# Weight pieces that are swapped inside a segment loop, loaded by one transfer or by two of half the columns

## The chip, the cores and the metric

The kernel runs on one core of a Trainium2 chip. The metric is the device time of one execution in microseconds (us). TensorE (PE) does the matrix products, VectorE (DVE), ScalarE (ACT) and GpSimd (POOL) the rest, and SyncE (SP) issues transfers, which 16 DMA engines carry out. The profile comes from one execution, recorded by the hardware profiler.

## What is computed

Two branches over the same input of 2048 tokens by 640 are mixed with a gate for each token, `g * a + (1 - g) * b`. Branch `b` is a gated feed-forward network. Branch `a` is attention with a recurrent memory: 64 segments of 32 tokens, where each segment's first 8 output rows are the memory of the next. Cut to what matters:

```python
mem = mem0
for s in range(n_seg):                       # 64
    h = jnp.concatenate([mem, xs], axis=1)   # 8 + 32 rows
    q, k, v = h @ Wq, h @ Wk, h @ Wv         # 640 -> 32 heads x 192, each
    p = softmax(mask(q @ k.T * scale))
    o = (p @ v) @ Wo                         # 32 x 192 -> 640
    mem = o[:, :M, :].copy()
    outs.append(o[:, M:, :])
```

The segments therefore run one after another, and each needs all four weight matrices (bf16, 7.5 MB each).

## The kernel before

**Stages.** First the feed-forward branch runs over four blocks of 512 tokens, and its result goes to DRAM (`b_scr`). Then six units of the so-called left part (the last 8 tokens of each segment, whose Q and K do not depend on the memory) are prepared, and then `segment(s)` runs 64 times.

**Pieces.** The weights are cut into pieces. A key `(m, o, k)` with m = 0, 1, 2 is a slab of Wq, Wk or Wv: 128 rows of the 640 (one k of KT = 5) by the 1536 columns of eight heads (an "octet", o = 0 to 3), 384 KB. A key `(3, p)` is one of 16 pieces of Wo, 128 by 1920, 480 KB. The 76 pieces together do not fit into the on-chip memory. So 13 pieces of octet 0 share their place (a "slot") with the same piece of octet 3, and Wo pieces 0, 1, 2 with 13, 14, 15 (`partner`, lines 545 to 552). Even segments go through octets 0, 1, 2, 3, odd ones through 3, 2, 1, 0. Within a segment the first octet's pieces are used first, and then their slots are loaded with the partner, which the same segment uses last and the next segment first. That is a swap. In every segment from 1 on, 16 pieces are swapped: 5 of Wk, 3 of Wq, 5 of Wv, 3 of Wo; in segment 0 there are eight.

**Order.** `PROG` (line 506) is the order of one segment, written out by hand: `("g", n, k)` are the projections of group n (`proj`, whose matmuls are recorded at L1046, and at L226 where the weights stay loaded), `sc`, `ex`, `pt`, `pv` the attention of one octet, `wo` the output projection (`wo_part`: L1206, and L1229 for the last octet), `lf`, `le`, `vb` the left part for later segments. After each item, `swap_loads(s, item)` (line 612) looks at the pieces just used and calls `load_piece` (line 597) for the partner of each that has one; the K pieces of the first group wait until that group's last item.

**Queues.** All transfers of the segment loop are issued by SP in the order in which the program adds them: the swaps (L599), the output of the segment before (`out_store`, L956), the next segment's input (`x_load`, L706), the next segment's left Q and K (`stg_load`, L935), the feed-forward result (`bz_load`, L947; every fourth segment also `bzl_load`, L952), stores of the left part (L895, L1276). An issue waits on SP until what it overwrites has been read; what stands behind it waits as well.

**Waits.** `_Sched.add` works out the dependencies from regions of memory. A transfer raises the semaphore of its slot by 16 when it has landed, and a matmul that reads a piece waits for the latest value that any write to an overlapping region will reach. `finalize` leaves out a wait that an earlier one on the same engine covers. Each projection matmul reads columns from the whole width of its piece: four matmuls of one piece, each with every fourth group of 32 columns (Q, K) or a quarter of the columns (V).

## Time and profile before

Three runs took 1762.07, 1763.03 and 1769.55 us; the median is 1763.03. The profiled execution's span is 1765.1 us.

| What | Value |
|---|---|
| Median of 3 runs | 1763.03 us |
| Span of the profiled execution | 1765.1 us |
| Mean granted TensorE clock | 0.994 of full speed |
| Feed-forward and preparation, until the first full segment | about 210 us |
| One segment | 22.4 to 27.8 us between first swaps |
| Moved by DMA | 499.57 MB, 283 GB/s over the span |
| Transfers of Wq, Wk, Wv, Wo in the whole run | 209, 335, 335, 205 |
| Median time from issue to landing of these | 5.4, 7.1, 9.1, 6.4 us |

In lines of the profile, a group of instructions is named by the line of the kernel that recorded it, its engine and its operands, `out<-in`; `arena` is the on-chip memory that holds all weights and working tiles, `ps` the accumulators. In the views of waits the columns are the waiting engine and line, whom it waited for, the total in us, how often, and the longest. In the views of the DMA engines the digits are the busy share of 40 equal slices of the window in tenths. In the timeline of SP the columns are the start in us, the time of the issues together, the line, and the number of issues merged into one row.

### The profile page before, as it was taken

Reading aid. Unit: us, or ns where it says so; the run is one execution under the profiler, and the core shown is the slowest. Engines: PE = TensorE matmul, PEld = TensorE weight load, DVE = VectorE, ACT = ScalarE, POOL = GpSimd, SP = SyncE. Lnnn points to the kernel's source line nnn. Section 1 sums busy time; section 2 is a strip of 40 time slices with the busy share of each in tenths; the row PEclk is TensorE's granted clock in tenths of the full one; section 3 lists DMA queues with packets and bytes.
Section 4 is the critical chain, followed back from the end, with each engine's and each line's share of the span. In section 5 each row is a group of like instructions: output and inputs, shape, how many; then the busy total and the mean of one; then the engine's idle time right before and its main releaser. Section 6 shows DMA issues by size and latency. Waiting matters only on the chain.

```text
span 1765.1 us, 80301 instructions
## 1 busy us (share of the span) xinstructions
PE 1623.9 (92%) x39162; PEld 809.5 (46%) x31501; DVE 960.0 (54%) x2932; ACT 802.8 (45%) x1835; POOL 320.0 (18%) x1099
## 2 busy tenths in 40 slices
PE   9999999999999999999999989999999998999887
PEld 4554444444444444454444444454444444454444
DVE  2222655556555655555555655555555655655554
ACT  3222544545444544444444544444444544445443
POOL 1100111111112112111212111111211121121211
PEclk9999999999999999999999999999999999999999
DMA  9814987888778887888788887879787886879776
GB/s 335 295 48 157 329 313 250 320 313 288 280 269 311 299 308 253 315 290 319 281 280 293 296 293 250 314 285 323 279 280 275 311 310 241 312 282 327 283 275 238
DMA packets 271311, 499.57 MB, mean 283 GB/s; under 512 B 105304, under 2 KB 132208, under 8 KB 270960
## 3 DMA queue, kind: packets, MB, share of 16 engines
q1 hardware_dynamic: 267832, 491.34, 78.3%
q8 instruction: 276, 4.52, 1.0%
q10 hardware_dynamic: 3128, 3.09, 0.6%
q14 instruction: 75, 0.61, 0.1%
HBM read 473.22 MB, written 21.11 MB: 280 GB/s over the span
## 4 chain that ended last, share of the span: by engine, by line
PE 71%; DVE 15%; DMA 6%; issue 4%; ACT 4%; DVEq 0%; SPq 0%; ACTq 0%
PE ps L1046 20%; PE ps L226 15%; PE ps L1206 8%; DMA arena<-in_A_Wo_dram 5%; PE ps L1177 3%; PE ps L804 3%; PE ps L801 3%; PE ps L884 3%; PE ps L1100 3%; PE ps L819 2%; PE ps L1087 2%; DVE ps L1114 2%; DVE arena L1112 2%; PE ps L1095 2%; PE ps L1229 2%
## 5 line engine op out<-in xcount | busy, mean ns | idle before, releaser
L1046 PE MATMUL ps<-arena 128*32 128x384 bf16 x9940 | 723.0, 329 | 42.4 <-DVE arena L1375 34.4
L226 PE MATMUL ps<-arena 128*32 128x384 bf16 x7680 | 595.4, 328 | 7.9 <-DVE arena L1215 3.5
L1046 PEld LDWEIGHTS ps<-arena 128*32 128x32 bf16 x9940 | 257.5, 97 | 365.3 <-issue 226.0
L1080 DVE STREAM_TRANSPOSE arena<-arena 128x384 bf16<-128x384 bf16 x512 | 270.8, 557 | 150.8 <-ACT arena L1066 149.2
L1066 ACT ACTIVATE arena<-ps 128x384 bf16<-128x384 f32 x512 | 236.2, 489 | 211.6 <-PE ps L1046 196.3
L1206 PE MATMUL ps<-arena 128*32 128x320 bf16 x6144 | 293.6, 301 | 13.9 <-issue 13.4
L1124 ACT ACTIVATE ps<-ps 104x160 f32<-104x160 f32 x256 | 71.9, 281 | 293.4 <-DVE ps L1114 293.4
L1206 PEld LDWEIGHTS ps<-arena 128*32 128x32 bf16 x6144 | 163.5, 97 | 74.0 <-issue 19.4
L1112 DVE TENSOR_REDUCE arena<-ps 104x4 f32<-104x160 f32 x256 | 83.0, 324 | 165.8 <-PE ps L1100 164.6
L941 POOL COPY arena<-arena 128x96 bf16<-128x96 bf16 x256 | 70.3, 275 | 513.4 <-PE ps L1100 444.2
L1188 ACT ACTIVATE arena<-ps 128x480 bf16<-128x480 f32 (+1 forms) x256 | 137.0, 535 | 43.8 <-PE ps L1179 39.6
L1196 POOL COPY arena<-arena 128x96 bf16<-128x96 bf16 x256 | 68.3, 267 | 441.1 <-ACT arena L1188 357.3
L1162 ACT ACTIVATE arena<-ps 128x448 bf16<-128x448 f32 x192 | 104.2, 543 | 96.7 <-PE ps L1149 96.4
L1069 ACT ACTIVATE arena<-ps 128x384 bf16<-128x384 f32 x256 | 125.1, 489 | 20.9 <-PE ps L1046 16.3
L1177 PE MATMUL ps<-arena 128*64 128x160 bf16 x1536 | 123.1, 243 | 12.5 <-ACT arena L1162 6.9
L1126 DVE TENSOR_REDUCE arena<-ps 104x4 f32<-104x160 f32 x256 | 83.0, 324 | 92.5 <-ACT ps L1124 92.5
L1177 PEld LDWEIGHTS ps<-arena 128*64 128x64 bf16 x1536 | 80.8, 109 | 91.6 <-issue 31.7
L884 PE MATMUL ps<-arena 128*32 128x384 bf16 x1280 | 111.4, 330 | 2.2 <-issue 2.0
L1179 PE MATMUL ps<-arena 128*64 128x64 bf16 x1536 | 104.8, 193 | 4.1 <-issue 4.1
L891 DVE STREAM_TRANSPOSE arena<-arena 128x384 bf16<-128x384 bf16 x128 | 73.7, 576 | 31.6 <-ACT arena L889 27.8
L1215 DVE TENSOR_TENSOR arena<-ps,arena 64x160 f32<-64x160 f32 x160 | 50.8, 317 | 72.3 <-ACT arena L1212 61.6
L1114 DVE TENSOR_TENSOR ps<-ps,arena 104x160 f32<-104x160 f32 x256 | 85.0, 332 | 8.8
(84 smaller groups left out, 1819.2 us busy)
## 6 DMA issues: line engine op xcount, KB each, us to landing
arena<-in_A_Wk_dram SPq DMA_DIRECT2D x335, 384.0 KB, 7.1
arena<-in_A_Wv_dram SPq DMA_DIRECT2D x335, 384.0 KB, 9.1
arena<-in_A_Wo_dram SPq DMA_DIRECT2D x205, 480.0 KB, 6.4
arena<-in_A_Wq_dram SPq DMA_DIRECT2D x209, 384.0 KB, 5.4
arena<-left_qk_scratch SPq DMA_DIRECT2D x126, 96.0 KB, 2.8
left_qk_scratch<-arena SPq DMA_DIRECT2D x49, 192.0 KB, 2.3
left_qk_scratch<-arena SPq DMA_DIRECT2D x30, 96.0 KB, 5.7
ffn_b_scratch<-arena ACTq DMA_DIRECT2D x16, 160.0 KB, 4.4
```

Of the source, the lines that this page charges most:

```text
L226: return e.add_instruction(mybir.InstMatmult(name=nm, start_tensor_calc=like["start"], stop_tensor_calc=stop, tile_size=(128, 32), tile_po ...
L884: fns.append(lambda e, outp=outp, rhs=rhs, j=j: e.matmul(outp, lhs, rhs, start=(k == 0), stop=(k == KT - 1), tile_position=(0, 32 * j)))
L1046: fns.append(lambda e, outp=outp, rhs=rhs, j=j: e.matmul(outp, lhs, rhs, start=(k == 0), stop=(k == KT - 1), tile_position=(0, 32 * j)))
L1066: S_.add("act", lambda e, m=m, bk=bk: e.activation(out=rows_sb[m], in_=ps[:, bk, 0:384], func=ACTF.Copy), reads=[r_ps[bk]], writes=[r_rows ...
L1069: S_.add("act", lambda e, i=i, bk=bk: e.activation(out=v_sb[i % NVB].rearrange("p (c n) -> p c n", c=3), in_=ps[:, bk, 0:384].rearrange("p ...
L1080: S_.add("dve", lambda e: e.transpose(out=dst[:, :, 0:L], in_=rows_sb[m].rearrange("p (c r) -> p c r", r=L)), reads=[r_rows[m]], writes=[r ...
L1112: S_.add("dve", lambda e: e.tensor_reduce(out=mxs, in_=S3, axis=AX.X, op=ALU.max), reads=[rb], writes=[rst], name="smax max")
L1114: S_.add("dve", lambda e: e.tensor_tensor(out=S3, in0=S3, in1=mxb, op=ALU.subtract), reads=[rb, rst], writes=[rb], name="smax sub")
L1177: return [lambda e: e.matmul(full, v[:, e0:e0 + 64], PTm[:, i], start=True, stop=False, tile_position=(0, 64 * i), skip_group_check=True), ...
L1179: lambda e: e.matmul(part, vl[:, e0:e0 + 64], PTl[:, i], start=False, stop=True, tile_position=(0, 64 * i), skip_group_check=True)]
L1188: S_.add("act", lambda e: e.activation(out=apx(u[:, 0, 0, :], [[R, na], [3 * R, 4], [1, R]]), in_=ps[:, A, 0:na * W].rearrange("p (c t r) ...
L1206: fns.append(lambda e, i=i, t=t, j=j, gv=gv: e.matmul(ps[32 * j:32 * j + 32, bank, 0:2 * DJ].rearrange("p (h n) -> p h n", h=2), lhs2[i], ...
```

## The change

`load_piece` is called for the first loads (`"res"`) and for the swaps (`"swap s..."`). The first loads stay as they are. A swap is now two transfers with the same semaphore, one for each half of the piece's columns; each half has a region of its own, half as wide, so a reader of the piece depends on both. For Wo the two inner dimensions (3 x 640) are flattened to 1920 columns first. A half's row in one partition is 1536 bytes for Wq, Wk and Wv (3072 before) and 1920 bytes for Wo (3840 before).

```diff
     def load_piece(key, name):
         loaded[slot_id[key]] = key
-        S_.add("sp", lambda e: e.dma_start(piece_view(key, res_off[key]), piece_src(key)), writes=[r_res[key]],
-               dma_sem="slot%d" % slot_id[key], name="%s %s" % (name, key))
+        if not name.startswith("swap"):
+            S_.add("sp", lambda e: e.dma_start(piece_view(key, res_off[key]), piece_src(key)), writes=[r_res[key]],
+                   dma_sem="slot%d" % slot_id[key], name="%s %s" % (name, key))
+            return
+        n = piece_size(key) // 2
+        dst, src = bview(res_off[key], 2 * n), piece_src(key)
+        if key[0] == 3:
+            src = src.rearrange("p c n -> p (c n)")
+        for x in range(2):
+            S_.add("sp", lambda e, x=x: e.dma_start(dst[:, n // 2 * x:n // 2 * (x + 1)], src[:, n // 2 * x:n // 2 * (x + 1)]),
+                   writes=[sreg(res_off[key] + n * x, n)], dma_sem="slot%d" % slot_id[key], name="%s %s %d" % (name, key, x))
```

## The prediction

> **What bounds the kernel now.** I read the page first (busy shares, chain), then the DMA queues over the segment loop, then who waits for a weight load, and last the order of one segment on SP's queue. By "late" I mean time against the schedule of before.

> ```profile
> span 1765.1 us, 80301 instructions
> PE 1623.9 (92%) x39162; PEld 809.5 (46%) x31501; DVE 960.0 (54%) x2932; ACT 802.8 (45%) x1835; POOL 320.0 (18%) x1099
> ...
> PE 71%; DVE 15%; DMA 6%; issue 4%; ACT 4%; DVEq 0%; SPq 0%; ACTq 0%
> ```

> The span is TensorE's: it is busy for 92% of it and fills 71% of the chain. A load enters the chain with 6% only. So a slower load costs nothing until it lands after the matmul that wants it. The next view (busy time by stretches, the segment loop alone; the last two columns are DMA share and GB/s) shows how near that is, and the waits of TensorE's weight loads and matmuls show that it already happens:

> ```profile
> 228.00:1765.00 1537.00, 1404.86 (x36808) 700.77 (x29456) 881.47 (x2754) 728.02 (x1696) 295.18 (x1026) 0.99 0.81 290
> ```

> ```profile
> PEld ps L1229 <- DMA arena<-in_A_Wo_dram: 8.6, 12, 2.5
> PEld ps L1046 <- DMA arena<-in_A_Wk_dram: 2.0, 5, 0.7
> PEld ps L1046 <- DMA arena<-in_A_Wv_dram: 0.4, 1, 0.4
> ```

> The 16 DMA engines are 81% busy on average in the loop, and PE waits about 11 us in all for weights, mostly for the third Wo piece, the last swap of a segment. In one segment the DMA share by slices, and SP's issues, stand like this:

> ```profile
> DMA  5488999999999999999999999999999999977430
> ...
> q1 hardware_dynamic: 3153, 6.93, 91.1%
> ```

> ```profile
> 918.86 0.33 SPq L599 DMA_DIRECT2D arena<-in_A_Wk_dram  x1
> 919.36 1.29 SPq L599 DMA_DIRECT2D arena<-in_A_Wq_dram  x3
> 920.69 1.92 SPq L599 DMA_DIRECT2D arena<-in_A_Wk_dram  x4
> 922.66 2.51 SPq L599 DMA_DIRECT2D arena<-in_A_Wv_dram  x4
> 925.21 0.57 SPq L956 DMA_DIRECT2D out_dram<-arena  x1
> 925.83 0.51 SPq L706 DMA_DIRECT2D arena<-x_scratch  x1
> 926.38 1.00 SPq L599 DMA_DIRECT2D arena<-in_A_Wv_dram  x1
> 930.89 1.84 SPq L599 DMA_DIRECT2D arena<-in_A_Wo_dram  x3
> ```

> The reader is to see that 13 pieces of 384 KB are issued in 8.5 us, while the engines work them off until about 937, without a gap; the three Wo pieces join the end of the same backlog. From the trace's landing times, the median distances from landing to first use are, by s % 4: for the fifth V piece 2.60 / 1.01 / 0.91 / 1.91 us (s%4 = 0, 1, 2, 3), for the third Wo piece 1.81 / 0.04 / 0.50 / 2.57 us. 0.04 is a matmul that waited. So half of the segments have no slack, the other half about 2 us.

> **The change, part by part.**

> *Packets.* Every swap (8 in segment 0, 16 in each of the 63 others: 1016 transfers) becomes two. The bytes stay. Each transfer has one packet for each of 128 partitions, 8 to an engine, and one 4-byte semaphore packet to an engine. The medians of the trace's packet records are 9 ns for 4 bytes, 36 for 768, 55 for 1280, 121 for 3072 and 149 for 3840. From 3072 to 3840 the slope is 28 / 768 = 0.0365 ns a byte, and a line through 3072 leaves 121 - 112 = about 8.5 ns that do not depend on the size (768 bytes: 28 + 8.5 = 36.5, agrees). No packet of 1536 bytes is in the trace; by the line it takes 64.5 ns, bounds from the nearest rows 55 (1280) and 121 / 2 = 60.5 (no fixed part) below, 72 (the 95th percentile at 1280) above. A piece then costs 8 x 8.5 + 9 = 75 to 77 ns more on each engine; I take 75. The bounds give 9 ns (only the semaphore) and 8 x 23 + 9 = 190 ns. That the packets are really back to back is seen in the backlog: landings of 384 KB pieces are 0.95 to 0.98 us apart, and 8 x 121 + 9 = 977 ns. Thus by the last V piece (the 13th) the engines are 13 x 0.075 = 0.98 us late, by the third Wo piece 16 x 0.075 = 1.2 us.
> [...]

> *Issues.* SP issues 16 more transfers in a segment. The second half has no wait of its own: it writes what the same matmuls released, and both raise the slot's one semaphore, for whose last value the matmul waits. An issue of a swap takes 0.436 us (median of 992 in the loop) or 0.528 (mean; the long ones lie mainly where nine and more transfers are outstanding), and 0.045 to the next. Whether a half costs the median or the mean decides which is slower, SP or the engines. From the first Wk issue to that of the last V half there are 25 intervals plus out store and x load (0.57 + 0.51 + 0.09 = 1.17 us): 25 x 0.481 + 1.17 = 13.2 us, or 25 x 0.573 + 1.17 = 15.5. A first piece lands 3.93 us after its issue (mean of 62 segments), 2.95 more than its own 0.98, so the last V half lands 13.2 + 2.95 + 0.53 = 16.7 or 19.0 us after the first issue. Before, it lands at 17.28 (mean), and the engines alone make that 18.26. So SP is hidden under the engines at the median and adds 19.0 - 18.26 = 0.74 us at the mean. I take the middle, 0.36: last V 1.33 us late, third Wo 1.56. What is queued behind on SP: the Wo swaps, then stg_load, bz_load, bzl_load, the left stores. Before, SP stands idle from 937.2 to 940.7 in the segment shown, so these slip by 1 to 2 us into idle time; POOL's fill of the next segment's Q and K has over 3 us until its scores. I cost them at nothing; without that cover they would add their lag beyond it, under 1 us a segment.

> *The sum.* Per segment, PE is pushed by the largest of (lateness - slack) over its 16 pieces, and the next segment starts afresh, because its first swap is released by PE itself. Over the 62 segments from 230 us on, with each segment's own slacks: s%4 = 1: 22.6 us in 15 segments; s%4 = 2: 17.4 in 16; s%4 = 3: 1.2; s%4 = 0: 2.8; together 44 us. Engines alone give 31, SP at the mean 60. The remaining segment adds 1. Against it stands the fetch of instructions (below): -4 of a possible 0 to -9. Following the lateness through SP's whole order from segment to segment, instead of piece by piece, gave 45 at issues of 0.45 us and 61 at 0.52; I lean on it and take +49 before the fetch, **+45 in all**. On this execution's 1765.1 us that is 1810. The execution lies 2.1 us above the median of the runs (1763.03), so the runs should show **1808**.

> **Rivals.**

> [...]

> 2. *SP becomes the bound.* If the halves' issues average 0.60 us, the last V half lands at 25 x 0.645 + 1.17 + 3.48 = 20.8 us, 3.5 late; less the mean slack of 1.62 that is 1.9 us x 62 = 117 us, 1880. It decides from 0.50 us an issue on, where SP's sum passes the engines' 18.26. For it: one in ten issues takes over 0.74 us. Against: those stand mostly behind a deep backlog, which shrinks when SP is slower.

> [...]
> [...]

> That the change does nothing is excluded by the changed program's order on SP: 128x768 and 128x960 transfers in pairs in every segment.

> **How the numbers follow.** Forecast (1794 to 1824, engines alone to SP at its mean) 0.62; rival 1 (1765 to 1790) 0.18; rival 2 (1825 to 1950) 0.15; rival 3 0.05. About 0.5% (9 us) is what a measurement of this kernel can tell from no change. A third of rival 1 lies within that, so same 0.07; faster 0.04 from rival 3 (a part of it ends as same); slower 0.89. For 8 in 10, 7% of rival 1 and rival 3 are left out below and the dearer half of rival 2 above: 1776 to 1868.

> **What would show it.** Packets of 1536 bytes at 64 to 65 ns in the records and q1's share in the loop up from 0.81 by 16 x 0.075 / 24.8 = 5 points, less what the longer span takes back; the DMA slices full to the end of a segment; L1229 and L1046 waiting for Wo and Wv some 40 us longer, in s%4 = 1 and 2 above all; the median of the halves' issues near 0.44 us. Wrong would be: waits for weights unchanged (rival 1), DMA slices with gaps inside the burst and every segment longer (rival 2), or fetch gaps gone (rival 3).

## The result, and the profile after

The changed kernel takes 1864.18 us (median of 4 runs, 1858.10 to 1868.33) against 1762.55 us for the kernel before (4 runs, 1761.58 to 1769.55). The ratio is 1.0582, with a 95% interval of 1.0549 to 1.0616: 101.6 us slower, where 45 were predicted. Line numbers below L597 have moved by 9: L599 is now L608, L1046 is L1055, L1206 is L1215, L1229 is L1238, L1375 is L1384.

From the page of the profiled execution (span, busy times, and the DMA queue of the swaps):

```profile
span 1859.7 us, 81317 instructions
...
PE 1666.8 (90%) x39162; PEld 800.9 (43%) x31501; DVE 962.5 (52%) x2932; ACT 804.2 (43%) x1835; POOL 322.4 (17%) x1099
...
q1 hardware_dynamic: 414136, 491.40, 81.1%
```

TensorE has the same 39162 instructions and is busy 42.9 us longer (1623.9 before). The busy time by stretches, for the segment loop alone, has the granted clock in the third column from the end:

```profile
228.00:1859.70 1631.70, 1447.65 (x36840) 693.25 (x29484) 885.21 (x2757) 731.22 (x1700) 297.63 (x1027) 0.97 0.84 274
```

The clock went from 0.99 to 0.97 and the DMA share from 0.81 to 0.84. What the matmuls of the loop wait for, from the views of waits (waiting engine and line, for whom, us in total, times, longest): first the main line for weights in the kernel before, then the kernel after.

```profile
PE ps L1229 <- DMA arena<-in_A_Wo_dram: 6.1, 10, 2.3
```

```profile
PE ps L1238 <- DMA arena<-in_A_Wo_dram: 57.9, 67, 2.0
PE ps L1055 <- DVE arena L1384: 30.7, 47, 0.8
...
PE ps L1055 <- DMA arena<-in_A_Wv_dram: 21.9, 31, 2.2
PE ps L1055 <- DMA arena<-in_A_Wk_dram: 14.6, 27, 2.2
```

The matmuls' waits for weights are 57.9 + 21.9 + 14.6 = 94.4 us (95.0 with Wq) in 126 gaps, where they were 6.6 us in 12 (6.1 for Wo, 0.5 for Wk). The waits for DVE are about as before. One segment of the changed kernel on SP, with the 16 DMA engines over 995.1 to 1018.1 us:

```profile
995.10 0.91 SPq L608 DMA_DIRECT2D arena<-in_A_Wk_dram  x2
996.05 2.80 SPq L608 DMA_DIRECT2D arena<-in_A_Wq_dram  x6
998.90 4.60 SPq L608 DMA_DIRECT2D arena<-in_A_Wk_dram  x8
1003.54 3.76 SPq L608 DMA_DIRECT2D arena<-in_A_Wv_dram  x8
1007.35 0.58 SPq L965 DMA_DIRECT2D out_dram<-arena  x1
1007.97 0.52 SPq L715 DMA_DIRECT2D arena<-x_scratch  x1
1008.53 1.04 SPq L608 DMA_DIRECT2D arena<-in_A_Wv_dram  x2
1009.62 3.79 SPq L608 DMA_DIRECT2D arena<-in_A_Wo_dram  x6
```

```profile
DMA  0679897999999999999998999999897899999711
...
q1 hardware_dynamic: 5341, 6.91, 89.4%
```

The 26 halves of Q, K and V take SP from 995.1 to 1009.6, 14.5 us where it was 8.5, and the digits now have sevens and eights inside the burst. Over the 62 full segments of the loop, the packets take 0.90 of the 16 engines' time between 3 and 6 us after a segment's first Wk issue; it was 0.98 before, and it is 1.01 in `packets` below (packets overlap a little, before up to 17.6 at a time on the 16 engines as the mean of 1 us, so a full burst can read above 1). The engines' backlog behind SP is smaller: the last V piece lands 4.3 us after its last issue, and it was 9.0. It is not gone, for the first half of a burst lands 2.7 us after its issue. In this segment the Wo halves stand on SP directly behind the V halves, without the gap of 3.5 us that the timeline of before shows.

The profiled executions differ by 1859.7 - 1765.1 = 94.6 us. The gaps of TensorE in the loop and its busy time account for most of it, +92 us together:

| Term | Before | After | Difference |
|---|---|---|---|
| Matmuls waiting for weights | 6.6 us | 95.0 us | +88 |
| TensorE busy (same instructions) | 1623.9 | 1666.8 | +43 |
| Gaps that end after an instruction packet | 32.2 (45 gaps) | 2.2 (3 gaps) | -30 |
| Waits for DVE and ACT | 77.1 | 68.5 | -9 |

The mean segment grew from 26.14 / 24.06 / 23.37 / 25.13 us (s % 4 = 0, 1, 2, 3) to 27.30 / 26.46 / 25.24 / 25.65.

**The second term is the clock.** In after there are 24 stretches with a granted clock of 0.5, 99.3 us together; before had 6 of 23.6 us. They are 3.4 or 6.8 us long, but for the last one of each run, which lies behind the last matmul. TensorE works for 88.3 us of them in after, and for 19.4 before. One of them, by stretches of 3.4 us (columns: length, busy time of PE, PEld, DVE, ACT, POOL, granted clock, DMA share, GB/s):

```profile
1042.30:1045.70 3.40, 1.15 (x47) 0.55 (x36) 1.21 (x4) 0.69 (x2) 0.19 (x1) 0.99 0.48 163
1045.70:1049.10 3.40, 3.40 (x48) 0.82 (x24) 1.17 (x4) 0.03 (x1) 1.50 (x4) 0.50 0.33 91
1049.10:1052.50 3.40, 3.40 (x90) 1.07 (x42) 1.95 (x5) 1.41 (x4) 0.54 (x2) 1.00 0.85 252
```

In the first stretch TensorE stands idle for 3.40 - 1.15 = 2.25 us. In the next it runs without a pause and completes 48 instructions, and in the one after it 90 in the same time. The 23 stretches of after that slow any matmul follow one in which TensorE was idle for 1.42 to 2.63 us. So much idle time does not always do it. Of the 3.4-us stretches at full rate in the loop of after, none of 292 with less than 1.4 us of idle time was followed by half rate, 10 of 20 with 1.4 to 1.8 us, and all 12 with more. The 88.3 - 19.4 = 68.9 us more of work at half rate cost half of that, 34 of the 43 us.

### The profile page after: what moved, and what is told of

Same layout as the page of the kernel before. It is cut to its first block, busy times and chain, and to the rows that moved or that the text cites. A ratio compares the mean times of both kernels' runs of the same rounds, so it can differ in the third digit from the quotient of the medians.

```text
span 1859.7 us, 81317 instructions
## 1 busy us (share of the span) xinstructions
PE 1666.8 (90%) x39162; PEld 800.9 (43%) x31501; DVE 962.5 (52%) x2932; ACT 804.2 (43%) x1835; POOL 322.4 (17%) x1099
## 5 line engine op out<-in xcount | busy, mean ns | idle before, releaser
L1055 PE MATMUL ps<-arena 128*32 128x384 bf16 x9940 | 745.1, 337 | 71.3 <-DVE arena L1384 31.4
L226 PE MATMUL ps<-arena 128*32 128x384 bf16 x7680 | 616.1, 339 | 9.6 <-DVE arena L1224 3.5
L1055 PEld LDWEIGHTS ps<-arena 128*32 128x32 bf16 x9940 | 259.4, 99 | 439.8 <-issue 240.2
L1089 DVE STREAM_TRANSPOSE arena<-arena 128x384 bf16<-128x384 bf16 x512 | 270.6, 557 | 168.6 <-ACT arena L1075 168.5
L1215 PE MATMUL ps<-arena 128*32 128x320 bf16 x6144 | 283.0, 300 | 0.0
L1215 PEld LDWEIGHTS ps<-arena 128*32 128x32 bf16 x6144 | 157.8, 97 | 54.5 <-issue 1.1
L1238 PE MATMUL ps<-arena 128*32 128x160 bf16 x3072 | 84.1, 238 | 66.3 <-DMA arena<-in_A_Wo_dram 59.6
L893 PE MATMUL ps<-arena 128*32 128x384 bf16 x1280 | 108.4, 330 | 0.0
L1238 PEld LDWEIGHTS ps<-arena 128*32 128x32 bf16 x3072 | 53.6, 97 | 117.2 <-DMA arena<-in_A_Wo_dram 76.7
```

The source lines that it names most:

```text
L226: return e.add_instruction(mybir.InstMatmult(name=nm, start_tensor_calc=like["start"], stop_tensor_calc=stop, tile_size=(128, 32), tile_po ...
L893: fns.append(lambda e, outp=outp, rhs=rhs, j=j: e.matmul(outp, lhs, rhs, start=(k == 0), stop=(k == KT - 1), tile_position=(0, 32 * j)))
L1055: fns.append(lambda e, outp=outp, rhs=rhs, j=j: e.matmul(outp, lhs, rhs, start=(k == 0), stop=(k == KT - 1), tile_position=(0, 32 * j)))
L1089: S_.add("dve", lambda e: e.transpose(out=dst[:, :, 0:L], in_=rows_sb[m].rearrange("p (c r) -> p c r", r=L)), reads=[r_rows[m]], writes=[r ...
L1215: fns.append(lambda e, i=i, t=t, j=j, gv=gv: e.matmul(ps[32 * j:32 * j + 32, bank, 0:2 * DJ].rearrange("p (h n) -> p h n", h=2), lhs2[i], ...
L1238: S_.add("pe", [lambda e, j=j, c=c, g_=g_, p=p: e.matmul(ps[32 * j:32 * j + 32, OB2, SC:512], u[:, p % 4, c, 0:L], g_[:, c, DJ * j:DJ * (j ...
```

## The experiments

Each ratio is against the kernel before on the same chip, with its 95% interval, and the us are differences of medians. "Late" means against the schedule of before, counted from the segment's first Wk issue.

### Packets without issues, and issues without smaller packets

`packets` issues each swap once and asks for each row in two packets. It leaves out the last 16 columns of each half, 2% of the bytes:

```diff
-        for x in range(2):
...
+        dst, src = [v.rearrange("p (x n) -> p x n", x=2)[:, :, 0:n // 2 - 16] for v in (dst, src)]
+        S_.add("sp", lambda e: e.dma_start(dst, src), writes=[r_res[key]],
...
```

> One transfer for each swap, as before the change, but each partition's row in two packets of 1504 bytes (Wo: 1888), so packets are doubled and SP's issues are not; the last 16 columns of each half are left out (2% of the bytes). Theory P (the extra packets make the loads late): mean packet times of the changed kernel (72.9 ns at 1536 bytes against 132.4 at 3072) make a piece 8 x (2 x 72.9 - 132.4) = 107 ns dearer, less 19 ns for the bytes left out, so the third Wo piece comes about 1.4 us late: waits for weights 35 to 45 us longer, time +40 to +70 us. Theory S (SP's extra issues make them late): time within +15 us of before, waits for weights under 20 us.

Measured: 1.0148 (1.0118 to 1.0178), +27.8 us, between the ranges of the two theories. The DMA queue, and the waits in the loop:

```profile
q1 hardware_dynamic: 397880, 483.01, 80.8%
```

```profile
PE ps L1215 <- issue: 12.8, 13, 1.7
PE ps L1055 <- issue: 10.4, 16, 1.3
PE ps L1238 <- DMA arena<-in_A_Wo_dram: 8.1, 16, 0.8
```

The queue carries packets by the number of after (398 thousand against 414) and nearly its share, but the waits for weights are 9.6 us in all, 3 more than before. The gaps with no wait of TensorE's own ("issue") grew from 32.2 us in 45 to 47.2 us in 66; each of them ends 1.0 to 1.7 us after a 16 KB instruction packet, as before (1.2 to 1.6 us). The last V piece lands 17.92 us after the first Wk issue, 0.64 later than before. TensorE is at half rate for 16.3 us, no more than before. So smaller packets alone cost a quarter of the loss. Only 3 us of that are waits for weights; 15 us are longer gaps after instruction packets, and 5 us are busy time of TensorE (1629.1 us).

`issues` keeps the rows whole and splits by partitions:

```diff
-            S_.add("sp", lambda e, x=x: e.dma_start(dst[:, n // 2 * x:n // 2 * (x + 1)], src[:, n // 2 * x:n // 2 * (x + 1)]),
+            S_.add("sp", lambda e, x=x: e.dma_start(dst[64 * x:64 * x + 64, :], src[64 * x:64 * x + 64, :]),
...
```

> Two transfers for each swap, but split by partitions (64 and 64) and not by columns: SP issues as often as in the changed kernel, packets keep 3072 and 3840 bytes and their number. Theory S: most of the 101 us comes back, time +60 to +100 us. Theory P: only the 16 extra semaphore packets of 9 ns for each engine and segment are left, time +0 to +15 us, waits for weights under 20 us. Both a part: in between, and then this run and the one with packets alone should add up to about +100.

Measured: 1.3069 (1.3050 to 1.3088), 2303.5 us, far above both expectations. The queue's line tells why:

```profile
q1 hardware_dynamic: 284088, 491.40, 87.4%
```

87.4% of a span of 2300.0 us is more engine time than before (78.3% of 1765.1), for the same bytes in nearly as many packets. The packets of 3072 bytes took a median of 199 ns where they take 121 in a transfer of 128 partitions, those of 3840 took 258 where they take 149. The packets were made slower, so this run says nothing on issues alone. That was settled later, by `after_cut`: the changed kernel with the columns that `packets` leaves out, so both move the same packets and the same bytes, and only the number of transfers differs.

```diff
-            S_.add("sp", lambda e, x=x: e.dma_start(dst[:, n // 2 * x:n // 2 * (x + 1)], src[:, n // 2 * x:n // 2 * (x + 1)]),
+            S_.add("sp", lambda e, x=x: e.dma_start(dst[:, n // 2 * x:n // 2 * (x + 1) - 16], src[:, n // 2 * x:n // 2 * (x + 1) - 16]),
```

> The changed kernel with the last 16 columns of each half left out, so its packets (1504 and 1888 bytes) and bytes are those of the run with packets alone, and only the issues of SP are doubled against that run. Theory S (most of the cost is that SP, issuing twice, no longer builds up a backlog): time +80 to +105 us, that is 55 to 80 us more than with packets alone. Theory P (the packets; the run with packets alone was cheap because of the 2% of bytes it left out): time +20 to +40 us.

Measured: 1.0551 (1.0512 to 1.0591), +97 us. Its waits:

```profile
PE ps L1238 <- DMA arena<-in_A_Wo_dram: 64.7, 76, 2.1
...
PE ps L1055 <- DMA arena<-in_A_Wv_dram: 28.1, 35, 2.8
...
PE ps L1055 <- DMA arena<-in_A_Wk_dram: 5.9, 17, 0.9
```

These are the waits of after (98.7 us here, 95.0 there), and the last V piece lands at 19.11 us, as in after (19.14) and 1.19 later than in `packets`. So of about 97 us, 97 - 28 = 69 come with the second transfer of each piece, at the same packets and bytes. This pair is the cleanest of the study. It does not tell which part of a second transfer costs the time, its issue on SP or its own way to the landing. The 28 us of `packets` are not simply a term of the 97 either: the gaps after instruction packets, over half of the 28, are 1.1 us in `after_cut`.

### Which pieces, and which segments

`qkv_only` splits the 13 Q, K and V swaps, `wo_only` the three Wo swaps:

```diff
-        if not name.startswith("swap"):
+        if not name.startswith("swap") or key[0] == 3:
```

> The Wq, Wk and Wv swaps are split, those of Wo are not (13 of 16 pieces). Lateness at the last V piece as in the changed kernel (1.9 us), at the third Wo about 0.6 us less than there (SP issues six times fewer, three pieces keep their packets). By the slack of each segment that leaves 50 to 70 of the 88 us of waits: time +55 to +80 us. If the Wo pieces' own splitting were the cause: time +0 to +20 us.

> Only the three Wo swaps of a segment are split. They come at the end of the backlog and gather 3 x 0.12 = 0.36 us: by the slack of each segment 7 us of waits, time +5 to +15 us. If the Wo pieces' own splitting were the cause: time +60 us and more.

In `qkv_only` the matmuls still wait for Wo above all:

```profile
PE ps L1238 <- DMA arena<-in_A_Wo_dram: 61.9, 78, 2.7
```

Measured: `qkv_only` 1.0618 (1.0596 to 1.0639), +110 us; `wo_only` 0.9933 (0.9909 to 0.9957), -11.7 us. Both expectations were missed, on opposite sides. The sum, 98, is the whole change (101.6). So the wait is at the Wo pieces, but its cause lies in the 13 pieces issued ahead of them: it is what TensorE waits for last, and not what was made dear. `wo_again` is the same kernel as `wo_only`, with more runs:

> The kernel with only the Wo swaps split, once more with five rounds: it was 0.7% faster than before in three. If that is real, the ratio lies again between 0.990 and 0.997 with an interval below 1, and PE's gaps that follow an instruction fetch without a wait of its own are again fewer than the 45 (32 us) of before. If it was chance, the interval holds 1.

Measured: 0.9953 (0.9934 to 0.9971), 1757.43 against 1764.87 us. The gain stands, about half a per cent, and this is the fastest version of the study. One packet-side rival for it was tried, `wo_packets` (the edit of `packets`, for Wo alone):

> Only the Wo swaps, in one transfer each with each partition's row in two packets of 1888 bytes (the last 16 columns of each half left out, 1.7% of three pieces): the packets of the kernel with only Wo split, without its extra issues. If the 0.5 to 0.7% gain seen there comes from the smaller packets, the ratio is 0.990 to 0.998 with an interval below 1; if it comes from the extra issues or from where instruction fetches happen to fall, the interval holds 1.

Measured: 0.9979 (0.9958 to 0.9999), -5.1 us. Its matmuls wait 5.2 us for weights in the loop (before 6.6); the gaps after instruction packets are 27.8 us in 44 (before 32.2 in 45, `wo_again` 25.6 in 41). The interval only just excludes no change and overlaps that of `wo_again`, so whether the Wo halves gain by their packets or by their second issue stays open.

`seg12` splits only in segments with s % 4 = 1 or 2, where the prediction found little slack, and `seg03` only in the others:

```diff
-        if not name.startswith("swap"):
+        if not name.startswith("swap") or int(name[6:]) % 4 in (0, 3):
```

> Swaps are split only in segments with s%4 of 1 and 2, which had 0.04 to 1 us of slack. Slack theory: 69 of the 88 us of waits stay, and with the clock time +65 to +90 us. If the cost were the same in every segment: +50 us.

> Swaps are split only in segments with s%4 of 3 and 0, which had about 2 us of slack. Slack theory: 19 of the 88 us of waits, time +10 to +30 us. If the cost were the same in every segment: +50 us. The two runs should add up to about +100 if segments do not act on each other.

Measured: `seg12` 1.0443 (1.0419 to 1.0467), +79 us; `seg03` 1.0128 (1.0106 to 1.0149), +23 us. The sum is 102, the whole change: in sum, what a segment loses does not depend on whether its neighbours were changed, which bears out "the next segment starts afresh". More than three quarters lie where the slack was smallest.

### More issues, the packets as they were

`tiny` is the kernel before, with a transfer of 512 bytes behind each swap, from one place of DRAM to another:

```diff
+        if name.startswith("swap"):
+            i = len(tiny)
+            tiny.append(i)
+            S_.add("sp", lambda e: e.dma_start(t_scr[i], w_gate[0:16, 0:16]), writes=[Rg("dt", i, i + 1)],
+                   dma_sem="tiny%d" % (i % 4), watch=True, name="tiny %d" % i)
```

`packets_tiny` is `packets` with the same addition.

> The kernel before, with one transfer of 16 x 16 numbers from one place of DRAM to another issued by SP behind each swap: SP's issues are doubled as by the change, weights and their packets are as before (each engine gets one packet of some 10 ns and one semaphore packet of 9 ns more for each swap, 0.3 us a segment). Theory S (the extra issues carry most of the cost): waits for weights over 50 us, time +60 to +110 us. Theory P: the time stays within +20 us. Both needed together (a slower issue alone is hidden by the backlog that SP builds, more packets alone are hidden by the slack): within +35 us here, although packets alone gave +26 us.

> Halved packets in one transfer (as in the run with packets alone, the last 16 columns of each half left out) and the small transfer behind each swap: the two halves of the change, put together from separate parts. If packets and issues are all there is, the time is +85 to +125 us, with 75 to 110 us of waits for weights and 80 to 130 us at half clock. If splitting by columns has a cost of its own (landing in two steps on one semaphore, or the order of the halves), it stays under +70 us.

Measured: `tiny` 1.1494 (1.1455 to 1.1532), +267 us; `packets_tiny` 1.1581 (1.1545 to 1.1616), +279 us; both are far above what was expected. SP's timeline in `tiny`:

```profile
1000.93 0.58 SPq L601 DMA_DIRECT2D arena<-in_A_Wk_dram  x1
1001.55 0.49 SPq L606 DMA_DIRECT2D tiny_scratch<-in_B_w_gate_dram  x1
1002.09 0.58 SPq L601 DMA_DIRECT2D arena<-in_A_Wk_dram  x1
```

From one Wk issue to the next are 1.16 us, longer than the 0.98 us that the engines need for a piece, and q1 is busy for 75.5% of the span only. SP is the bound here, and the last V piece lands at 20.82 us. The added transfer is dearer than a half (0.49 + 0.58 us for a piece against 2 x 0.43), so the run does not size the change; it shows the mechanism of rival 2, and how steep it is. `packets_tiny` adds only some 12 us to `tiny`, where the same packets cost 28 us alone. In both runs no gap after an instruction packet is left, and those were over half of the 28; that the engines' extra time is hidden once SP is behind is a likely reading too, and was not isolated.

### The clock

`pulse3` and `pulse7` are the kernel before, with nothing in its loads changed. In each segment 3 or 7 small copies on POOL stand behind the third of the five steps of one projection group, and the next step's matmuls wait for them (the line that adds the copies):

```diff
+                if item == ("g", 3, 2):
+                    for _ in range(3):
+                        S_.add("pool", lambda e: e.tensor_copy(out=ident, in_=ident),
+                               reads=[r_ident], writes=[r_ident, r_zz], name="pulse s%d" % s)
```

> The kernel before, with PE made to wait once in each segment, after the third of the five matmul steps of group 3, for three copies on POOL that it does not need otherwise (some 1.2 to 1.5 us; no load is touched). Clock theory (a window of about 3.4 us in which PE idles 1.4 us or more is followed by one at half clock): a stop below that threshold costs its own length, 64 x 1.2 to 1.5 = 77 to 96 us, less what it gives back in waits that would have come later, and adds under 30 us at half clock. Rival (the half clock has another cause, or costs nothing): the same.

> As pulse3 with seven copies, a stop of some 2.6 to 3.2 us. Clock theory: in most segments one window idles for more than 1.4 us, so the time at half clock rises to 64 x 3.4 x 0.6 = 130 us or more, PE's busy time rises by half of that (65 us), and the step from pulse3 to pulse7 is 64 x 1.4 to 1.7 us of stop (90 to 110 us) plus 40 to 65 us. Rival: the step is the stops' own length, PE's busy time stays at 1624 us within 10.

Measured: 1.0338 (1.0313 to 1.0364), +60 us, and 1.1228 (1.1188 to 1.1268), +214 us. The segment loop of `pulse3`, then of `pulse7`, by busy time and clock:

```profile
228.00:1828.00 1600.00, 1400.41 (x36848) 692.59 (x29488) 887.87 (x2757) 734.79 (x1700) 352.35 (x1213) 1.00 0.79 279
```

```profile
228.00:1969.00 1741.00, 1469.67 (x36974) 709.81 (x29606) 890.08 (x2767) 737.57 (x1706) 422.29 (x1462) 0.95 0.74 257
```

`pulse3` adds 67 us of idle time to the loop (1600.00 - 1400.41 = 199.6, before 1537.00 - 1404.86 = 132.1), 1.1 us a segment, and TensorE's busy time does not grow: 8.9 us are at half rate, and only 3.4 of them hold any matmuls. `pulse7` adds another 72 us, and now the same work keeps TensorE busy 69 us longer, with 182.2 us at half rate, 165.8 of them with matmuls. In the loop of `pulse3`, 23 stretches have between 1.4 and 2 us of idle time, and one is followed by half rate. In `pulse7` it is 3 of 34 with 1.4 to 1.8 us, and all 35 with more. Over the loops of all 17 traces, 2 of 5125 stretches with less than 1.4 us of idle time were followed by half rate, 150 of 388 with 1.4 to 1.9 us, and all 197 with more. So in these traces a wait that brought the idle time of a stretch above 1.9 us was paid again in slower matmuls, and one that left it under 1.4 us was not, but for the 2. What decides in between was not found.

How much of the +43 us of busy time in after lengthened its end is another question, since slower matmuls also give a late load time to land. `fill_after` puts 48 short matmuls (about 1.1 us) ahead of the last octet's output projection in the segments with s % 4 = 1, into an accumulator that the next one overwrites; `fill_before` does the same to the kernel before.

```diff
+        if lasto and pairs[0] == allp[0] and s % 4 == 1:
+            p, g_, rg_ = held[0]
+            S_.add("pe", [lambda e, j=j, g_=g_, p=p: e.matmul(
+                ps[32 * j:32 * j + 32, OB2, SC:512], u[:, p % 4, 0, 0:L], g_[:, 0, DJ * j:DJ * (j + 1)],
+                start=True, stop=True, tile_position=(0, 32 * j)) for _ in range(12) for j in range(4)],
+                reads=[rg_, r_uT[ub]], writes=[r_ps[OB2]], name="fill s%d" % s)
```

> The changed kernel, with 48 short matmuls (some 1.1 us) put ahead of the last octet's Wo matmuls in segments with s%4 = 1, where PE waits 1.5 us on average; they use a piece that is always there, and their result is overwritten. If windows at half clock cost time at the end: the time at half clock falls by 20 us or more in these segments and the time falls by 5 to 15 us against the changed kernel's 1864, although PE has 18 us more to do. If the half clock only fills waits for loads: time the same or up to 5 us longer.

> The same 48 matmuls in the kernel before, where PE waits there only some 0.3 us on average: they cost their own length less that wait, 16 x 0.8 = 13 us, +8 to +18 us.

Measured: `fill_after` 1.0536 (1.0506 to 1.0565), `fill_before` 1.0066 (1.0038 to 1.0094), +10.9 us. In `fill_after` the time at half rate fell from 99.3 to 47.1 us, TensorE's work within it from 88.3 to 39.4, and TensorE was busy for 1657.6 us, less than in after (1666.8) in spite of more matmuls. The ratio's interval touches that of after (1.0549 to 1.0616), so at most it can be said that the filler, which costs 10.9 us where nothing is to be gained, costs nothing or gains a little there. By the medians (1857.2 against 1864.2 us), 10.9 + 7 = some 18 of the 24 us that 49 us of work at half rate stand for reached the end; the uncertainty of that is as large as the 7.

## Why the prediction was right in direction and too small

**The price of a packet was right, and the 28 us of `packets` agree by luck.** 1536-byte packets took a median of 65 ns, predicted 64.5. In `packets` the last V piece was 0.64 us late, and the 16 columns that it leaves out in each half save 16 x 32 x 0.0365 = 19 ns a piece, 0.24 us over 13: 0.88 us, predicted 0.98. The prediction's sum for the engines alone was 31 us, less 4 for the fetch, and `packets` measured 28. But the 31 were to be waits for weights and the fetch was to get cheaper, while `packets` waits 3 us more for weights and 15 us more after instruction packets. The packet medians of after (65 ns at 1536 bytes, 79 at 1920) agree with the line through the rows of before (64.5 and 78.6), and `after_cut` shows that the bulk of the loss was never in the packets' price.

**The step that failed is the term for SP's halves: when they are issued, and how long after that they land.** "Whether a half costs the median or the mean decides which is slower, SP or the engines [...] I take the middle, 0.36." The prediction put the long issues down to nine and more transfers outstanding, and so could expect them to go as the backlog shrinks. In the trace of before only 32 of the 126 swap issues over 0.7 us had so many. Most of the long ones go with something else: 69 of the 126 overlap in time with a 16 KB instruction packet on q8, while 45 of the 695 of up to 0.5 us do. In after it is 172 of 178 against 81 of 1732. The 267 issues that overlap such a packet take 1.026 us on average in after, the others 0.436. That the instruction packet is what holds the issue up is inferred from this overlap and was not tried by itself. With twice as many issues more of them were hit, 267 where it was 142. So the backlog shrank and the median was 0.432 us, but the mean stayed at 0.515 (before 0.528). The last V half was issued 14.85 us after the first Wk issue, 0.5 us behind the middle of the prediction's two sums (13.2 and 15.5).

The rest of the lateness lies between issue and landing. The prediction let the last half land 2.95 + 0.53 = 3.48 us after its issue, as the first piece of a burst does; it took 4.29. So the last V half landed at 19.14 us, 1.86 late, predicted 1.33, and the third Wo piece about 2.5 us late, predicted 1.56. That the prediction's formula gave 19.0 at the mean of before is in part luck: at the mean interval of after (0.515 + 0.043) it gives 25 x 0.558 + 1.17 + 3.48 = 18.6, and the engines alone give 18.26. The landing is later than either sum, so SP and the engines are not rivals of which only the slower one counts. The 8th piece shows it best: it was 1.38 us late, where 8 x 0.075 = 0.6 were reckoned. Its second half was issued at 8.00 us, sooner than SP's sum at the mean has it (15 x 0.573 = 8.6), and landed 5.42 us after its issue. Engines that run short of halves early in the burst (0.90 of their time, against 1.01 in `packets`) and build up a queue later would do that; how the two add up was not isolated.

**The table of slacks was right in sum, not in its spread.** With the measured lateness in place of the predicted one it gives some 87 us of waits, and the trace has 88 more. Waits were to lie in s % 4 = 1 and 2 above all. Counted from each segment's first swap they are 8.7 / 48.5 / 16.9 / 19.8 us (s % 4 = 0, 1, 2, 3), where the table with the measured lateness has 11 / 36 / 32 / 7. So s % 4 = 1 is the largest as predicted, but s % 4 = 3, reckoned at 1.2 us, came out above 2, and the larger lateness explains only a part of it. That the total agrees is luck to that extent, and the cause of the spread stays open. In `packets` the same table gives 11 us with the measured lateness, and 3 more were waited.

**A term was missing: the clock.** The sum counted a wait at its own length. In this kernel a wait is dearer when it brings TensorE's idle time in one 3.4-us stretch to between 1.4 and 1.9 us or above, since the next 3.4 us of matmuls can then run at half rate. The slow stretches of after follow 1.42 to 2.63 us of idle time in sum; the longest single gap at a matmul in its loop is 2.2 us. Before, 6 stretches at half rate were there to be seen, hidden in a mean clock of 0.99. The term is +43 us of busy time. `pulse7` shows that it can lengthen the end: its step from `pulse3` is 153 us, of which 72 are idle time and 69 busy time; how much of the 43 us did so here is open, as `fill_after` could not size it.

**The fetch was wrong in size and in cause.** The gaps after instruction packets went from 32.2 to 2.2 us where 4 were allowed for. The 4 us were the author's estimate for a 16 KB instruction packet that is through sooner among smaller weight packets, and no run shows it: the packet's mean time was 1.043 us before, 1.073 in after, and 1.090 in `packets`, which has the small packets and 47.2 us of these gaps. In the trace of before it was no shorter where hardly any weight packets were under way (a median of 1.064 us for the 29 packets of the loop with less than one of them at a time on average, 1.008 for the 121 with 15 and more). The gaps remain in `packets` and `fill_before` (41.6 us), where TensorE hardly waits for weights, and vanish where it does. A likely reading is that the instructions arrive while TensorE waits for something else. `pulse7` bears it out: its loads are those of before, its matmuls wait for POOL and hardly for weights (1.4 us), and these gaps are down to 1.3 us in 3. `pulse3` lies between, with 15.3 us in 22, and `tiny`, with whole packets, has none. So smaller packets are not what removes them.

```profile
PE ps L1047 <- POOL arena L1306: 173.8, 62, 2.9
...
PE ps L1047 <- issue: 0.8, 1, 0.8
```

Two of the largest groups of these gaps before, and the largest that is left in after:

```profile
PE ps L1206 <- issue: 12.7, 13, 2.0
...
PE ps L1046 <- issue: 5.0, 7, 1.3
```

```profile
PE ps L1238 <- issue: 1.1, 1, 1.1
```

**The rivals.** Rival 1 (hidden, 1765 to 1790 us) falls with the waits of 95 us. Its range took a split piece for cheaper than the forecast's 75 ns on each engine, and no run shows that: by the medians of after it is 8 x (2 x 65 - 121) + 9 = 81 ns. Rival 2 (SP becomes the bound) has the right mechanism at less than its price: it named 0.50 us an issue as the point from which it decides, the mean was 0.515, and both of its signs came, gaps of the DMA engines inside the burst and a longer segment of every kind. Rival 3's sign came too, the fetch gaps are gone but for 2.2 us, but beside longer waits and in a slower kernel.

From the predicted 45 us to the measured ones: the waits are 88 and not 49 (+39), the clock was left out (+43, if all of it reached the end), the fetch gave 30 and not 4 (-26). That makes 101, beside 94.6 between the two profiled spans, where the waits for DVE and ACT give back another 9, and 101.6 between the medians of the runs.

## What to carry to other kernels

Where transfers are issued back to back, compare the issuing engine's mean time for an issue, not its median, with the time that the DMA engines need for a transfer: SP at 0.515 us on average, 0.56 from issue to issue, was fast enough for pieces of 0.98 us and not for halves of 0.53 us. A wait names the load that is late last, and the cause may stand far ahead of it in the queue: here the wait was at Wo, splitting Wo was free, and splitting Q, K and V cost all of it. Before a wait on TensorE is priced, add up its idle time in stretches of 3.4 us and look for a granted clock of 0.5 behind the ones with more than 1.4 us (here always there above 1.9), for a mean clock of 0.99 does not show them.
